# A recurrence and its mixture of experts on one core: step orders written out, the first expert in two passes, four tails in one block

## The chip, the core and the metric

The kernel runs on one core of a Trainium2 chip. A core has TensorE (matmuls; PE in the profile, its weight loads PEld), VectorE (DVE), ScalarE (ACT), GpSimd (POOL) and SyncE (SP), each with an instruction queue of its own that is worked off in order. Data moves by DMA; SP, ACT and POOL start transfers. The metric is the device time of one execution in microseconds (us). A profiled execution also has a span, from its first to its last instruction.

## The reference

The first part is a recurrence over 768 positions for 4 x 8 heads of dimension 40, the second a mixture of eight experts over the 3072 rows that come out, each row going to one expert.

```python
for t in range(S):
    y[:, :, t] = np.einsum('bhd,bhde->bhe', rt, state)
    Sa = np.einsum('bhde,bhe->bhd', state, at)
    state_decay = state * wt[:, :, None, :] - np.einsum('bhd,bhe->bhde', Sa, bt)
    state = state_decay + np.einsum('bhd,bhe->bhde', vt, kt)
...
logits = x @ w_gate                      # x: (3072, 320), 8 experts
expert_idx = np.argmax(logits, axis=1)
...
for e in range(E):                       # rows of one expert
    h = np.maximum(x_sorted[lo:hi] @ w1[e], 0.0)   # 320 -> 1024
    y_sorted[lo:hi] = h @ w2[e]                    # 1024 -> 320
return gate_w[:, None] * y
```

All arithmetic is float32. The inputs come from a fixed seed.

## The kernel before

**Units.** The recurrence is cut into 12 chunks of 64 positions, and the heads into two groups (two of the four batches each). One chunk of one group is a unit: 24 units, numbered in order, and unit u + 2 takes its state from unit u. `unit(u)` (L617) doesn't issue instructions but records steps, each with an engine, what it reads and writes, and a name.

The steps of a unit, by name and engine:
- loads of six inputs, 4 DMA starts each: the decay rows `dec`, then B, K, A, R, V (L642; on ACT for B, A and R of unit 0, on SP otherwise)
- DVE `scan_r` (L658), `recip`, `scan_q` (L664): running products of the decay; POOL `decay_kb` (L670, two) and `decay_a` (L672) apply them to K, B and A
- PE `p_a` (L686): products of the 64 positions with each other; DVE `n1` (L695) masks one half, ACT `gt` and POOL `gt_mask` (L700) the other, DVE `t1` (L716) transposes
- an inverse by doubling: PE `p_sq`, `p_sum2`, `p_sum4`, `p_sum8`, `p_last`, with DVE transposes `x0`, `x02`, `x04`, `x08`, ACT copies `x1`, `x12`, `x14` and sums `s2` (POOL, L720, four), `s4`, `s8` (DVE, L733); each product needs the one before it. The last step into the tile TT is an ACT copy `kept` (three instructions) and a POOL addition `tt_add` (L792)
- PE `p_q`, `p_rhs` (reads the state), `p_u1`, `p_first`, ACT `first`, PE `p_u2`, ACT `minus`, PE `p_z`, DVE `zu` (L907), PE `p_y` (L930, the `ZU,nKB` matmuls), DVE `sa` and POOL `st` (L839, the state for unit u + 2), DVE `xt` (L940)
- PE `p_x` (L953) turns the result to rows and multiplies with the gate's weights; `logits`, `exp`, `weight`, `scaled`, `xs_pad`, and a `store` of the 128 rows to memory. PE transposes are `t_kb`, `t_v`, `t_gt`, `t_st`, `t_u`.

**Order.** `in_order` (L364) issues the steps, greedily, by a planner's costs and ready times. For units 2 to 22 a table `CYCLE` (L312) gives each step a place relative to its unit's number, and each engine but SP takes the steps in the order of these places. Units 0, 1 and 23 and all other steps are placed by the planner.

**Routing.** `route(c0, c1)` (L1011) handles one or two chunks: `choose` (first smallest logit), `p_count` (two f32 matmuls that count rows per expert), `place` (a slot for each row), `one_hots`, `p_table` and an addition to the table `tab` of rows by slot. It is on POOL, and on DVE for the last chunks. After the last chunk `by_count` sorts experts 1 to 7 by their counts, `in_places` reorders the table, and `rows_at` (L233) turns slots into row indices for gathering and scattering. Work on an overflow of rows follows in a branch that runs only if an expert has more rows than its capacity.

**Experts.** An expert's pass has a first layer (`layer1`, 24 matmuls over its columns, that is rows of x; eight of them half as high and run in pairs) and a second (`layer2`, 8 matmuls of 320 columns for each block of 128 rows). Expert 0 runs inside the step planner with the last units: 384 rows gathered by `rows_in` (L1165), transposed by `p_rows` (L1170), first layer, output passes and `rows_out`. Its 64 further rows come with expert 1. Experts 1 to 7, sorted by falling count, have 448, 416, 416, 416, 416, 384 and 384 columns. The rows over 384 are tails; two experts' tails share an output pass (`layer2` with two parts, side by side in the output's partitions), in three shared passes. Weights of the next expert are fetched while one runs; three rooms take turns.

The capacities are in one line:

```python
TAIL = (64, 64, 32, 32, 32, 32, 0, 0)
```

Of the kernel before, what the change touches and what calls it, by code (L numbers as in the profile page):

```python
# [23 lines left out]
def kernel(  # L24
# [23 lines left out]
    nc = tc.nc  # L48
# [27 lines left out]
    TAIL = (64, 64, 32, 32, 32, 32, 0, 0)  # L76
# [43 lines left out]
    before = consts.tile([128, 128], F32)  # L120
    ones_sq = consts.tile([128, 128], F32)
    zero_e = consts.tile([128, E], F32)
    iota_r = consts.tile([128, 128], F16)
    tokv = consts.tile([128, NT], F32)
# [10 lines left out]
    counted("off_b", [128, E], [[PJ * 128, E]], 0, to=offs[:])  # L135
# [7 lines left out]
    def route_constants():  # L143
# [12 lines left out]
        yield lambda: nc.gpsimd.tensor_copy(iota_r[:], iota_f)  # L156
        yield lambda: nc.gpsimd.tensor_copy(tokv[:, : NT // 2], tokc)
        yield lambda: nc.gpsimd.tensor_scalar(tokv[:, NT // 2 :], tokc, scalar1=-1.0, scalar2=None, op0=ALU.mult)
        yield lambda: nc.gpsimd.memset(ptr[:], 0.0)
# [6 lines left out]
    def fill_turn_gate(e):  # L166
        nc.gpsimd.memset(turn_gate[:, :, 2 * D :], 0.0)
        for p in range(NP):
            nc.gpsimd.tensor_copy(
                turn_gate[:, p, : 2 * D].rearrange("x (a d) -> x a d", a=2), ident[:].rearrange("x (a d) -> x a d", a=2)[:, :, :D],  # L170
            )

    def load_turn_gate(e):
        for par in range(2):
            nc.scalar.dma_start(
                turn_gate[par * HP : par * HP + D, :, 2 * D :], moe_w_gate.rearrange("(p a e) n -> a e p n", a=2, e=D)[par],
            )
# [7 lines left out]
    sel = rte.tile([128, NCH, BH, E], F32)  # L185
# [4 lines left out]
    g0_idx = rte.tile([128, NJ], I32)  # L190
    s0_idx = rte.tile([128, NJ], I32)
    g_idx = rte.tile([128, (E - 1) * PJ], I32)
    s_idx = rte.tile([128, (E - 1) * PJ], I32)

    key = rte.tile([128, E - 1], F32)
    over = rte.tile([128, E - 1, E - 1], F32)
# [5 lines left out]
    tab_o = rte.tile([128, (E - 1) * PJ], F32)  # L202

    def by_count():
        v = nc.vector
        v.scalar_tensor_tensor(key[:], in0=ptr[:, 1:], scalar=16.0, in1=iota_f[:, : E - 1], op0=ALU.mult, op1=ALU.subtract)
# [12 lines left out]
    def in_places():  # L219
# [6 lines left out]
        to = tab_o[:].rearrange("x (e j) -> x e j", j=PJ)  # L226
        v.tensor_reduce(to, perm_tab, axis=AX, op=ALU.add)
        v.tensor_copy(to[64:, 0, NJ : NJ + 1], to[:64, 0, NJ : NJ + 1])
        v.tensor_copy(to[:64, 0, NJ : NJ + 1], tab[:64, NJ : NJ + 1])
        for i in (1, 3):  # L230
            v.tensor_copy(to[32:64, i, NJ : NJ + 1], to[:32, i + 1, NJ : NJ + 1])

    def rows_at(v, t, tmp, gi, si):  # L233
# [5 lines left out]
        v.tensor_tensor(tb, tb, ta, op=ALU.add)  # L239
        v.tensor_copy(gi, tb)  # L240

# [1221 lines left out]
```

## Time and profile before

| | us |
|---|---|
| four runs | 698.13 to 705.74, median 702.66 |
| the profiled execution, its own time | 697.83 |
| its span | 696.0 |
| PE busy in the span | 640.9 (92%) |
| PEld, DVE, ACT, POOL busy | 501.5, 389.0, 283.0, 383.8 |
| mean granted TensorE clock | 0.994 of full speed |

Busy times of different engines overlap. The end of a matmul is modelled in the profile, so a busy PE isn't PE at its peak. The first `p_x` (unit 0) starts 58.2 us into the span, those of units 2 and 20 at 91.27 and 394.68, the last at 435.63. Expert 1 begins at 469.25 and the last output pass at 674.92.

### The profile page before, as it was taken

Reading aid. Unit: us, or ns where it says so; the run is one execution under the profiler, and the core shown is the slowest. Engines: PE = TensorE matmul, PEld = TensorE weight load, DVE = VectorE, ACT = ScalarE, POOL = GpSimd, SP = SyncE. Lnnn points to the kernel's source line nnn. Section 1 sums busy time; section 2 is a strip of 40 time slices with the busy share of each in tenths; the row PEclk is TensorE's granted clock in tenths of the full one; section 3 lists DMA queues with packets and bytes.
Section 4 is the critical chain, followed back from the end, with each engine's and each line's share of the span. In section 5 each row is a group of like instructions: output and inputs, shape, how many; then the busy total and the mean of one; then the engine's idle time right before and its main releaser. Section 6 shows DMA issues by size and latency. Waiting matters only on the chain. (4 is left out here: it accounts for less than half of the span.)

```text
span 696.0 us, 32091 instructions
## 1 busy us (share of the span) xinstructions
PE 640.9 (92%) x13957; PEld 501.5 (72%) x13957; DVE 389.0 (56%) x850; ACT 283.0 (41%) x755; POOL 383.8 (55%) x575
## 2 busy tenths in 40 slices
PE   2688989999999999999999987989999999999995
PEld 2477888888889988888888886555746555665653
DVE  5578978888889988887887676701111202010110
ACT  2356656655556655655665654221011101111110
POOL 8788758896889788967895562023115021311101
PEclk9999999999999999999999999999999999999998
DMA  4422323333333333333232101337276019303000
GB/s 101 94 67 60 95 62 77 74 78 98 73 103 81 90 79 75 98 77 92 60 92 65 34 24 50 117 122 240 96 207 208 10 50 288 91 10 94 20 9 25
DMA packets 120212, 60.66 MB, mean 87 GB/s; under 512 B 100587, under 2 KB 115949, under 8 KB 120068
## 3 DMA queue, kind: packets, MB, share of 16 engines
q1 hardware_dynamic: 114696, 48.82, 26.7%
q0 software_dynamic: 2992, 9.25, 4.2%
q8 instruction: 111, 1.82, 1.1%
q10 hardware_dynamic: 2380, 0.50, 0.3%
q14 instruction: 33, 0.27, 0.1%
HBM read 49.88 MB, written 8.98 MB: 85 GB/s over the span
## 5 line engine op out<-in xcount | busy, mean ns | idle before, releaser
L1286 DVE TENSOR_SCALAR h_sb<-hp 128x416 f32<-128x416 f32 (+3 forms) x32 | 17.3, 542 | 188.6 <-PE hp L1281 164.2
L733 DVE TENSOR_TENSOR wx<-ps,wx 64x256 f32<-64x256 f32 (+1 forms) x216 | 90.4, 418 | 41.7 <-PE ps L606 31.4
L606 PE MATMUL ps<-wx 64*64 64x128 f32 (+1 forms) x3072 | 102.1, 266 | 7.5 <-ACT wx L595 1.7
L295 POOL DMA_INDIRECT out_dram<-zo,s_idx x24 | 23.6, 983 | 139.3 <-ACT zo L1303 138.1
L606 PEld LDWEIGHTS ps<-wx 64*64 64x64 f32 x3072 | 80.9, 136 | 19.5 <-issue 8.8
L720 POOL TENSOR_TENSOR wx<-T,ihalf 64x256 f32<-64x256 f32 x96 | 71.3, 743 | 30.5 <-DVE T L716 19.8
L595 ACT COPY wx<-ps 128x256 f32<-128x256 f32 (+2 forms) x124 | 52.2, 422 | 36.3 <-PE ps L606 23.1
L1297 PE MATMUL zp<-w,h_sb 128*128 128x320 f32 (+2 forms) x256 | 66.4, 433 | 0.0
L670 POOL TENSOR_TENSOR KB<-KB,rv 128x512 f32<-128x512 f32 x48 | 58.4, 1220 | 5.6 <-DMA R<-in_packed_dram 1.8
L766 DVE STREAM_TRANSPOSE wx<-ps 128x512 f32<-128x512 f32 x72 | 50.9, 707 | 8.9 <-PE ps L606 6.1
L1297 PEld LDWEIGHTS zp<-w,h_sb 128*128 128x128 f32 (+2 forms) x256 | 41.5, 172 | 18.7 <-issue 3.0
L1287 ACT ACTIVATE h_sb<-hp 128x416 f32<-128x416 f32 (+3 forms) x32 | 15.3, 477 | 93.3 <-PE hp L1281 48.0
L1303 ACT COPY zo<-zp 128x320 f32<-128x320 f32 (+1 forms) x24 | 10.2, 425 | 100.5 <-PE zp L1297 100.5
L1297 PE MATMUL zp<-wx,h_sb 128*128 128x320 f32 (+2 forms) x176 | 48.5, 433 | 0.0
L1273 PE MATMUL hp<-xgT,w 128*128 128x416 f32 (+1 forms) x128 | 46.8, 514 | 0.0
L792 POOL TENSOR_TENSOR TT<-TT,wx 128x512 f32<-128x512 f32 x24 | 34.6, 1442 | 20.6 <-ACT TT L595 18.1
L595 ACT COPY ZU<-ps 64x320 f32<-64x320 f32 x92 | 38.8, 421 | 5.5 <-PE ps L710 4.5
L710 PE MATMUL ps<-ident,Vu 128*128 128x128 f32 x184 | 30.0, 286 | 11.6 <-DMA Vu<-in_packed_dram 11.0
L1297 PEld LDWEIGHTS zp<-wx,h_sb 128*128 128x128 f32 (+2 forms) x176 | 30.9, 178 | 13.4 <-issue 2.6
L606 PE MATMUL ps<-ZU,nKB 128*64 128x104 f32 (+1 forms) x768 | 39.8, 254 | 0.7 <-DVE ZU L907 0.6
L700 POOL TENSOR_TENSOR GT<-GT,m_low 128x512 f32<-128x512 f32 x24 | 31.4, 1310 | 15.9 <-DVE wx L766 9.6
L1251 POOL DMA_INDIRECT xg<-x_rows,g_idx x20 | 19.2, 958 | 37.7 <-PE tp L1259 30.0
(248 smaller groups left out, 1366.5 us busy)
## 6 DMA issues: line engine op xcount, KB each, us to landing
KB<-in_packed_dram SPq DMA_DIRECT2D x188, 40.0 KB
w<-in_moe_w_dram SPq DMA_DIRECT2D x20, 320.0 KB
w<-in_moe_w_dram SPq DMA_DIRECT2D x10, 512.0 KB
x_rows<-xs SPq DMA_DIRECT2D x24, 192.0 KB
dec<-in_packed_dram SPq DMA_DIRECT2D x96, 40.0 KB
Vu<-in_packed_dram SPq DMA_DIRECT2D x96, 40.0 KB
wx<-in_moe_w_dram SPq DMA_DIRECT2D x12, 320.0 KB
A<-in_packed_dram SPq DMA_DIRECT2D x92, 40.0 KB
```

The source lines that it names most:

```text
L295: ins_ = nc.gpsimd.indirect_dma_start(out=out[:, :], out_offset=bass.IndirectOffsetOnAxis(ap=si, axis=0), in_=zo, in_offset=None, bounds_c ...
L595: nc.scalar.copy(dst, src)
L606: nc.tensor.matmul(out_, lhsT=lhsT, rhs=rhs, start=start, stop=stop, skip_group_check=True)
L670: Step(turn_of("decay_kb", pre), POOL, 1.57, lambda e, kb=kb, by=by: nc.gpsimd.tensor_tensor(kb, kb, by, op=ALU.mult), reads=hrv + hKB[2:] ...
L700: Step(turn_of("gt_mask", rk), POOL, 1.33, lambda e, d=dst_, m=mask: nc.gpsimd.tensor_tensor(d, d, m, op=ALU.mult), writes=held)
L710: nc.tensor.transpose(psum[:, ps.at, p * 128 : (p + 1) * 128], t[:, p].rearrange("x a j -> x (a j)"), ident[:])
L720: Step(turn_of("s2", rk + 0.5), POOL, 0.74, lambda e, z=z, par=par, q=q, X=X: nc.gpsimd.tensor_tensor(X[halves[par], q, :, 2, :], T1[halve ...
L733: nc.vector.tensor_tensor(dst[o_, q], src[o_, q], old[o, q], op=ALU.add)
L766: Step(turn_of(f"x0{k}", rk - 0.4), DVE, 0.72, lambda e, ps=ps, Xn=Xn: nc.vector.transpose(Xn[:, :, :, 0, :], half_sums(ps, 2)[:, :, :, 0, ...
L792: Step(turn_of("tt_add", rk - 1.5), POOL, 1.95, lambda e, X=X, TT=TT: nc.gpsimd.tensor_tensor(TT[:], TT[:], X[:, :, :, 2, :], op=ALU.add), ...
L1273: nc.tensor.matmul(hps[i][:, : c1 - c0], lhsT=w[0][:, db, (fb + i) * 128 : (fb + i + 1) * 128], rhs=xT[:, db, c0:c1], start=(db == 0 and n ...
L1297: nc.tensor.matmul(zp[r0 : r0 + n], lhsT=h[:, fb, c0 : c0 + n], rhs=w[2][:, fb, :], start=(fb == 0), stop=(fb == FB - 1), skip_group_check ...
```

## The change

- **Step orders.** `FIRST_STEPS` and `LAST_STEPS` write out, for each engine, SP included, the order of the steps of the first and of the last units, by step, part and unit (`s2/3:1` is the fourth part of `s2` of unit 1). All units take part (`FIRST_UNIT, LAST_UNIT = 0, 23`), `CYCLE` has new places for those between, and routing steps, stores, loads and weight fetches have names and places too.
- **Loads.** For units 0 and 1 half of `dec` is loaded by SP and half by ACT, B by ACT; R of unit 0 by ACT; the rest by SP. The gate's weights are loaded by SP instead of ACT.
- **Engines.** In units 0 to 3 DVE takes one of the two `decay_kb` and two of the four `s2`, in units 0 and 1 also `decay_a`. In the cycle one of two `nkb` goes from DVE to ACT and one of two `x12` from ACT to DVE. In units 0, 1, 22 and 23 TT is formed by DVE straight from PSUM (`direct`) instead of `kept` and `tt_add`.
- **First expert.** 256 of its rows, found in the first 8 of 12 chunks, run inside the planner (`NA = 2`, `EC = 8`); 192 more run as a second pass before expert 1. Eight gathers stand in the planner: two early, two for the second pass, four for expert 1.
- **Tails.** Experts 2 to 5 put their four tails of 32 rows in one block: one gather, one transposition, one `layer2` with four parts. Expert 2's second-layer weights get a tile of their own (`four_w2`), so that they last until expert 5. Expert 7 has 352 columns.
- **Routing.** Slots are placed with an offset per expert of 4096 and fewer operations; counts and selections are in f16 (`p_count`: one matmul and one more for each unit of the group). On DVE the counts are read straight from PSUM. `rows_at` is split into `rows_from` and `rows_to_`. The overflow bookkeeping moves behind expert 3's first layer (`left_over`).

The diff, cut to its core:

```diff
-    TAIL = (64, 64, 32, 32, 32, 32, 0, 0)
+    TAIL = (64, 64, 32, 32, 32, 32, 0, -32)
+    FOUR = range(2, 6)
+    NA = 2
+    EC = 8
...
-    FIRST_UNIT, LAST_UNIT = 2, 22
+    FIRST_UNIT, LAST_UNIT = 0, 23
+    FIRST_STEPS = {
+        PE: """
+            t_v:0 p_a:0 t_kb:0 t_gt:0 p_sq:0 p_a:1 p_sum2:0 t_kb:1 p_sq:1 p_sum4:0 t_v:2 p_rhs:0 p_sum2:1 p_sum8:0 t_v:1 t_gt:1 p_sum4:1 p_last:0
+            p_u1:0 p_first:0 p_q:0 p_sum8:1 p_a:2 p_u2:0 p_rhs:1 p_z:0 t_u:0 t_kb:2 p_last:1 p_sq:2 p_y:0 p_q:1 p_u1:1 p_sum2:2 p_first:1 p_x:0
...
+        DVE: """
+            zero_dec zero_dec/2 zero_dec/1 zero/5 zero/9 zero/10 zero/3 zero/7 zero/1 scan_r:0 scan_r:1 recip:1 decay_kb/1:0 recip:0 scan_q:0
+            decay_a:0 scan_r:2 decay_kb/1:1 n1:0 n1/1:0 t1:0 scan_q:1 decay_a:1 x0:0 s2/1:0 s2/3:0 n1/1:1 n1:1 t1:1 s2/4:0 x02:0 s2/3:1 s2/5:0
+            scan_r:3 x0:1 recip:2 s2/1:1 scan_q:2 x04:0 s4/1:0 s2/4:1 s4:0 x02:1 s2/5:1 s8/1:0 x08:0 s8:0 s4/1:1 direct:0 direct/1:0 s4:1 x04:1
+            decay_kb/1:3 decay_kb/1:2 scan_r:4 n1:2 n1/1:2 s8:1 s8/1:1 x08:1 zu:0 t1:2 zu/1:0 direct/1:1 recip:3 direct:1 s2/1:2 s2/3:2 x0:2 xt:0
...
+        ACT: """
+            first_load/3:0 first_load/1:0 first_load/1:1 pc:0 first_load/3:1 gt/1:0 gt:0 off/1:0 off:0 gk:0 nkb:0 x1:0 nkb/1:0 gt:1 v:0 gt/1:1 pc:2
...
+        SP: """
+            first_load:0 first_load:1 first_load/2:0 first_load/5:0 first_load/4:0 load:2 first_load/2:1 first_load/4:1 load:3 first_load/5:1
...
+    LAST_STEPS = {
+        PE: """
...
+            p_count:21 p_table:19 t_st:23 p_z:23 p_y:22 p_y:23 p_x:22 p_table:21 p_x:23 p_h/13 p_h/14 p_h/8 p_count:23 p_z0/8 p_h/9 p_h/10 p_z0/9
+            p_h/11 p_z0/10 p_table:23 p_z0 p_z0/1 p_h3/2 p_z0/2 p_h/15 p_h3/3 p_z0/11 p_z0/3 p_z0/4 p_z0/5 p_z0/6 p_z0/12 p_rows/3 p_z0/13 p_rows/4
+            p_z0/7 p_rows/5 p_rows/2 p_z0/14 p_rows/6 p_z0/15 p_rows/7
...
-    p_q -0.974  p_last -1.289  p_u1 -0.921  p_first -0.816  p_u2 -0.711  p_z -0.605  p_y -0.342   (places in CYCLE, PE)
+    p_q -0.500  p_last -0.786  p_u1 -0.357  p_first -0.310  p_u2 -0.214  p_z -0.024  p_y  0.167
-    tt_add -2.045  decay_kb -4.955 -5.591  gt_mask -3.136   (POOL)
+    tt_add -0.321  decay_kb -3.393 -3.179  gt_mask -1.250  choose 1.179  place 2.036  one_hots 3.107
...
+                on_ = DVE if spread and q else POOL
...
+                            nc.vector.tensor_tensor(TT[o, q], half_sums(ps, 1)[o_, q, :, 0, :], X[o, q, :, 2, :], op=ALU.add)
...
-                for i, m in enumerate((before, ones_sq)):
-                    mm(psum[:, ps.at, i * n * E : (i + 1) * n * E], m[:], sl_c.rearrange("p b e -> p (b e)"))
+                mm(t[:, :n], before[:], sl_c, stop=False)
+                for b in range(n):
+                    mm(t[:, b + 1 :], ones_sq[:], sl_c[:, b : b + 1].to_broadcast([128, n - b, E]), start=False, stop=b + 1 == n)
...
+    hs[0] = wk_pool.tile([128, FB, CAP - EW], F32, name="h_first", bufs=1)
+    layer1(weights[0], xTs[0], hs[0], EW, CAP, to=0)
+    layer2(rows_to(0, 0), (weights[0], hs[0], 0, 128))
...
+        if p == 1:
+            layer2(rows_to(p, NJ), (weights[0], hs[0], 128, 64), (w, h, MAIN, 64))
+        if p == 3:
+            left_over()
+        if p == FOUR[-1]:
+            layer2(rows_to(FOUR[0], NJ), *((weights[x], hs[x], MAIN, 32) for x in FOUR))
         for j in range(NJ):
-            layer2(rows_to(p, j), (w, h, j * 128, 128))
+            layer2(rows_to(p, j), (w, h, j * 128, min(128, MAIN + TAIL[p] - j * 128)))
```

## The prediction

> **What bounds the kernel now.** I read the table of busy time by stretch first, with cuts where the work changes. Each row is a stretch in us, its length, then the busy us (and instructions) of each engine, the granted clock and the DMA share.
>
> ```profile
> 0.00:91.27 91.27, 66.35 (x1881) 58.30 (x1881) 67.76 (x128) 43.52 (x111) 73.55 (x117) 0.98 0.36 83
> 91.27:394.68 303.41, 290.87 (x9827) 262.20 (x9825) 255.03 (x507) 186.51 (x513) 239.33 (x361) 1.00 0.33 79
> 394.68:436.73 42.05, 35.75 (x1268) 32.06 (x1263) 26.96 (x91) 19.50 (x55) 21.12 (x47) 1.00 0.14 41
> 436.73:469.25 32.52, 29.20 (x117) 18.23 (x115) 11.82 (x71) 8.06 (x22) 6.28 (x8) 1.00 0.38 122
> 469.25:674.92 205.67, 205.67 (x828) 121.74 (x829) 27.48 (x54) 23.68 (x52) 40.56 (x42) 1.00 0.36 112
> 674.92:696.00 21.08, 13.09 (x49) 8.94 (x47) 0.00 (x0) 1.77 (x4) 2.95 (x3) 0.89 0.06 22
> ```
>
> The cuts are the first matmul of `p_x` of units 2 and 20, the end of `p_x` of unit 23, and the first matmuls of expert 1 and of the last output pass. TensorE (first column) bounds it. It is never idle from 469.25 to 674.92, so work removed there shows one for one. In the middle it idles 12.5 of 303 us (a unit takes 16.86 us). The two joints are loose: 24.9 us idle in the first 91, and 6.3 + 3.3 = 9.6 us between 394.68 and 469.25. Next, the timeline of VectorE at the start (start, us, engine, line, operation; in brackets the idle time before it and what ended it).
>
> ```profile
> 6.33 1.24 DVE L658 TENSOR_TENSOR_SCAN rv<-dec,ones 128x521 f32<-128x521 f32 x1
> ...
> 15.58 1.30 DVE L658 TENSOR_TENSOR_SCAN rv<-dec,ones 128x521 f32<-128x521 f32 x1 [4.81 <-DMA dec<-in_packed_dram]
> ...
> 27.73 0.42 DVE L733 TENSOR_TENSOR wx<-ps,wx 128x256 f32<-128x256 f32 x1 [3.49 <-PE ps L606]
> ```
>
> Unit 1's decay rows land 9 us after unit 0's scan, because their load is sixth on SP. Then the waits of TensorE in the second joint (who waited for whom, total us, times, longest):
>
> ```profile
> PE ps L1170 <- DMA qini<-x_rows,g_idx: 3.0, 2, 2.1
> PE ps L606 <- ACT x L601: 1.1, 2, 0.6
> PE ps L606 <- DVE wx L766: 1.1, 1, 1.1
> ...
> PE ps L606 <- DVE xT L940: 0.9, 1, 0.9
> ```
>
> They are the serial steps of the last units and the gathers behind the routing. Last, TensorE's timeline in the expert stage:
>
> ```profile
> 489.23 1.10 PE L1273 MATMUL hp<-xT,w 128*128 128x64 f32 x8
> 490.17 0.82 PE L1259 MATMUL tp<-ident,xg 128*128 128x128 f32 x6
> ...
> 583.51 3.06 PE L1273 MATMUL hp<-xgT,wx 128*128 128x416 f32 x8
> 586.41 0.82 PE L1259 MATMUL tp<-ident,xg 128*128 128x128 f32 x6
> ...
> 629.38 0.43 PE L1297 MATMUL zp<-wx,h_sb 128*32 128x320 f32 x1
> 629.38 0.43 PE L1297 MATMUL zp<-w,h_sb 128*32 128x320 f32 x1
> 629.65 0.43 PE L1297 MATMUL zp<-wx,h_sb 128*32 128x320 f32 x1
> ...
> 644.63 2.85 PE L1273 MATMUL hp<-xgT,w 128*128 128x384 f32 x8
> 647.32 0.82 PE L1259 MATMUL tp<-ident,xg 128*128 128x128 f32 x6
> ```
>
> Start to start, a 416-column matmul instruction takes (586.41 - 583.51) / 8 = 0.362 us and a 384-column one (647.32 - 644.63) / 8 = 0.336: about 0.83 ns a column plus 0.016. Those of 64 columns take (490.17 - 489.23) / 8 = 0.117. The two 32-row tail parts start in the same instant and the next pair 0.27 us later, the same as one full 128-row matmul of the output pass: parts side by side cost one.
>
> **The sum, part by part.** It is made against the profiled execution: span 696.0 us, its own time 697.83.
>
> *Experts (idle-free).* A first-layer pass is 40 instruction slots (32 whole, 16 half-height ones in pairs). Expert 0 had 384 columns (13.4 us) and later 64 (485.19 to 490.17, 4.98). It gets 256 columns, 40 x (0.213 + 0.016) = 9.2, and 192, 40 x (0.160 + 0.016) = 7.0: -2.2 us; nothing is lost, since the output passes stay three and a shared one. Expert 7 goes from 384 to 352 columns: 40 x 32 x 0.83 ns = -1.1. One shared tail pass of 16 pair slots goes, 16 x 0.27 = -4.3, if four parts run side by side as two do. Only pairs are in this trace. Bounds: 0.268 a slot (the pair) and 4 x 0.11 = 0.44 (the weight loads of 128x32 take 0.11; none overlapping), so the four-part pass takes 4.3 to 7.0 and the term is -4.3 to -1.6. I take -4.3: the `ZU,nKB` pass, also 128 rows deep in column halves, does 16 pairs in 1.58 us, so two 128x64 loads fit in 0.1 us and four narrow ones fit in 0.27. One block of transposes less: 525.17 to 525.50, -0.3. Eight gathers instead of seven are turned in the joint: +0.4. Sum of the experts: -7.5.
>
> The Trainium skill ("TensorE: Matmul & The Clock Gate", Measured speedup vs the span model) gives three column tiles a speedup of 2.38 only, so four would not be free; by that efficiency (2.38 / 3) the pass would take an estimated 5.4 us and the term would be -3.2. The pairs of this trace show no such loss.
>
> The counts by expert, worked out from the seeded inputs, are 421, 323, 414, 388, 357, 423, 371, 375. Expert 0 has 293 in the first eight chunks, so 256 early rows are all real. Sorted, the others (423 down to 323) fit 448, four times 416, 384, 352. The overflow branch stays empty.
>
> *Start.* Loads of units 0 and 1 are split over SP and ACT, with unit 1's decay rows second on SP (four starts take 1.6 us there). VectorE takes over half the decay products, part of `s2` and the sum into TT, and becomes the queue that sets the pace. Its list up to `xt:0`, from rows of the profile: fills to 7.3 us; 8 scans x 1.3; 4 reciprocals x 0.2; 6 decay products, new there (0.67, the 128x512 product at L907; the same on POOL takes 1.22); 6 `n1` x 0.42; 9 transposes of T1, x02, x04, x08 x 0.71 and 3 of x0 x 0.68; 6 `s2` halves x 0.42; 8 sums x 0.41 and 8 x 0.86; `zu` 1.34; `xt` 0.69. That is 40.8 us: `p_x:0` at 48.8 with no wait, against 58.2. The lists to `xt:1` and `xt:2` add 11.7 and 18.5, so `p_x:2` comes at 79.0 with no wait, against 91.27: -12.3. VectorE waited 9.4 us for TensorE and 2.7 for ACT in the first 60 us; if all of that is paid again nothing is gained. I take just under half of it, 5.5: **-6.8** (bounds 0 and -12.3). The loads on two queues have no term of their own: one unit's 24 starts take 9.6 us of SP, which VectorE's fills cover to 7.3. ACT's half of unit 0's decay rows stands behind four starts of B, and those behind POOL's KB fill: to about 5.6 us, landing about 7.7, 0.4 late.
>
> *Middle.* A route's two count matmuls in f32 take 0.49 us (395.64 to 396.13). In f16 one more per unit of the group is issued; f16 instructions of 32 columns take 0.05 (four of `oh_c` in 0.19): 5 x 0.05, -0.2, five times -1.0. I summed TensorE's cyclic order in both versions with 15.2 us of pieces a unit. From the end of `p_first` to `p_u2` it has 0.6 us before and 0.9 after, from `p_u2` to `p_z` 0.9 before and 2.0 after; the weight loads waited 3.5 + 0.4 us there for ACT: -3.9. But from `p_last` to `p_q` the cover falls from 4.5 to 3.4 us. That chain is three ACT copies (1.1), possibly a `decay_kb` ahead on POOL (1.22), and `tt_add` (1.28): 2.4 to 3.6. What is queued behind a late `tt_add` is `gt_mask`, the second decay product and `st`, hence the next unit's `p_rhs`. Between 0 and 0.25 us a unit; I take half, +2.0. Middle: **-2.9** (bounds -12.5, all idle time gone, to +4.5).
>
> *Second joint.* Nine of sixteen `p_h` (2 x 0.229 us each) and two `p_h3` now stand among the steps of units 22 and 23: 5 us of filler for 6.3 us idle. Behind `p_x:23` 11.3 us of work stands ahead of `p_rows/3`. The routing there took 13.1 us from 436.83 to the index at 449.91. The DVE list drops 4 + 8 small operations of 0.2, the ACT hop of the counts (0.4) and the 2.6 us of overflow bookkeeping between `by_count` and `tab`; it adds the first index's 0.85 us and a copy: first index after 6.9 us, second after 9.7. Gathers go 1.28 apart and land 3.8 after issue (428.70 to 432.49) up to 6.2 with expert 1's weights in flight (450.65 to 456.89). `p_rows/7` is ready 17.6 to 20 us after `p_x:23`, with 15.6 of work: 2.4 to 4.8 idle, 1.0 more for the copies, and 0 to 3 left among the last units. I take 5.6 instead of 9.6: **-4.0** (bounds -6.5 to 0).
>
> Sum: -7.5 - 6.8 - 2.9 - 4.0 = -21.2. The profiled execution would go from 697.8 to 676.6. The four runs have a median of 702.66, 4.8 above it; I predict against that median: **681**.
>
> **Rivals.**
> - *The start gives nothing.* VectorE's added 4.0 us of decay products and 2.5 us of `s2` halves come while TensorE's pieces run at double length (`p_sum2:0` took 2.19 us, later ones 1.10), so all 12.1 us of waits return. For: those waits are serial steps, which an order can't shorten. Against: in the old order DVE stood idle meanwhile, with unit 1 not loaded. 681 + 6.8 = 688.
> - *The middle tightens.* Every unit falls to the 15.6 us of its pieces: another 9.6 of the 12.5 us idle goes, 671. Against: 10.4 of it is put down to issue, and the order does nothing to that.
> - *Slower: the POOL queue sets the period.* Place: `tt_add`, listed behind `decay_kb` and ahead of `gt_mask`. If `decay_kb` and a routing piece (one `one_hots` pair, 1.1) are both late, `p_q` waits 1.22 + 1.1 + 2.4 - 3.4 = 1.3 us; with `s2` late besides (0.74), 2.1. It is paid 18 times: 38, so 681 - 2 + 38 = 717. It decides from 1.3 us a unit (24 in all). For: POOL is busy 239 of 303 us, and its routing pieces are now fixed in the row. Against: those pieces average less than before, and POOL waited up to 4.8 us for `t1` just where they stand.
> - *The change hardly acts.* Idle time only moves from one hand-off to another, in the units and at both joints, and the experts' work alone goes: 702.7 - 7.5 = 695, or 698 with the four-part pass at its worst; 696 stands for it.
>
> The Trainium skill ("DMA: Bandwidth & Descriptors", Issuing engines are not separate DMA queues) says that issuing from two engines saves only the sequencer's time. By it the split loads do no more than the 0.4 to 1.6 us of issue here; the sum rests on their order anyway.
>
> **Chances.** Forecast 0.56, no gain at the start 0.17, tighter middle 0.12, slower 0.09, hardly acts 0.06. The range is 668 to 697: the low end is the tighter middle with a little more at the start, the high end the case that hardly acts; the four-part pass at its worst (+2.7) is inside. About 1% (7 us) is what a measurement of this kernel tells from no change. Below 695.6 lie the first three and a little of the last: faster 0.86, same 0.05, slower 0.09.
>
> **What would show it.** `p_x:2` near 84, not 91; the spacing of `p_x` near 16.7; idle TensorE between `p_x:20` and expert 1 near 5.6; four `128*32` parts starting together and 16 such groups in 4.3 us; the 352-column pass. A period over 17.5 with TensorE waiting for POOL's TT, or a first `p_x` after 56, would make it wrong.

## The result

| | median us | ratio to the kernel before, 95% interval |
|---|---|---|
| before (78 runs beside it) | 700.7 | 1 |
| after (52 runs) | 702.78 | 1.0017 [1.0001, 1.0033] |
| after, measured again in the experiments | 702.65 | 1.0032 [0.9999, 1.0066] |

The ratio leaves out the slow runs of both kernels, so it isn't quite the quotient of the medians. The forecast was 681, with a range of 668 to 697. The change leaves the time where it was. The profiled execution of the kernel after took 699.47 us, with a span of 697.7 and a mean granted clock of 0.975 (before: 697.83, 696.0 and 0.994).

### The profile page after: what moved, and what is told of

The parts are those of the page before. It is cut to its first block, busy times and chain, and to the rows that moved or that the text cites. A ratio compares the mean times of both kernels' runs of the same rounds, so it can differ in the third digit from the quotient of the medians.

```text
span 697.7 us, 32008 instructions
## 1 busy us (share of the span) xinstructions
PE 640.7 (92%) x13960; PEld 503.2 (72%) x13960; DVE 404.9 (58%) x868; ACT 278.6 (40%) x729; POOL 365.1 (52%) x504
## 4 chain that ended last, share of the span: by engine, by line
PE 46%; issue 30%; POOL 10%; DVE 4%; DMA 1%; ACT 0%; SPq 0%; POOLq 0%
PE ps L715 38%; PE ps L823 6%; POOL out_dram L310 3%; PE ps L944 3%; POOL xg L1396 2%; POOL KB L783 1%; POOL A L785 1%; POOL ST L960 1%; POOL GT L813 1%; POOL wx L833 1%; DMA KB<-in_packed_dram 0%; DVE q L776 0%; SPq L752 0%; PE hp L1418 0%; POOL qini L1301 0%
## 5 line engine op out<-in xcount | busy, mean ns | idle before, releaser
L833 POOL TENSOR_TENSOR wx<-T,ihalf 64x256 f32<-64x256 f32 x88 | 64.8, 737 | 43.1 <-DVE T L829 23.0
L783 POOL TENSOR_TENSOR KB<-KB,rv 128x512 f32<-128x512 f32 x44 | 67.3, 1529 | 15.5 <-DMA KB<-in_packed_dram 15.2
L704 ACT COPY wx<-ps 128x256 f32<-128x256 f32 (+2 forms) x104 | 44.2, 427 | 38.8 <-PE ps L715 17.9
L1449 ACT COPY zo<-zp 128x320 f32<-128x320 f32 (+1 forms) x24 | 10.2, 425 | 101.5 <-PE zp L1443 97.6
L1443 PE MATMUL zp<-wx,h_sb 128*128 128x320 f32 (+3 forms) x176 | 48.5, 434 | 0.0
L1443 PE MATMUL zp<-w,h_sb 128*128 128x320 f32 (+1 forms) x176 | 44.1, 433 | 0.0
L1443 PEld LDWEIGHTS zp<-wx,h_sb 128*128 128x128 f32 (+3 forms) x176 | 30.5, 176 | 13.8 <-issue 0.7
L913 POOL TENSOR_TENSOR TT<-TT,wx 128x512 f32<-128x512 f32 x20 | 26.9, 1346 | 24.1 <-ACT TT L704 20.0
L1418 PEld LDWEIGHTS hp<-xgT,w 128*128 128x128 f32 x128 | 23.7, 190 | 21.1 <-issue 17.1
L770 DVE TENSOR_TENSOR_SCAN rv<-dec,ones 128x521 f32<-128x521 f32 x24 | 37.5, 1566 | 1.8 <-DMA dec<-in_packed_dram 1.4
L1443 PEld LDWEIGHTS zp<-w,h_sb 128*128 128x128 f32 (+1 forms) x176 | 28.9, 176 | 13.2 <-issue 0.7
```

What stands on the lines that cost most here:

```text
L704: nc.scalar.copy(dst, src)
L770: Step(turn_of("scan_r", pre + 0.1), DVE, 1.3 if early else 1.55, lambda e: nc.vector.tensor_tensor_scan(rv[:, : SEG * C1 + 1][:, ::-1], d ...
L783: Step(turn_of("decay_kb", pre), on_, (1.2 if early else 1.35) if on_ == POOL else 0.6, lambda e, kb=kb, by=by: any_(e).tensor_tensor(kb, ...
L833: Step(turn_of("s2", rk + 0.5), DVE if spread and z else POOL, 0.4 if spread and z else 0.74, lambda e, z=z, par=par, q=q, X=X: any_(e).te ...
L913: Step(turn_of("tt_add", rk - 1.5), POOL, 1.6, lambda e, X=X, TT=TT: nc.gpsimd.tensor_tensor(TT[:], TT[:], X[:, :, :, 2, :], op=ALU.add), ...
L1418: nc.tensor.matmul(hps[i][:, : c1 - c0], lhsT=w[0][:, db, (fb + i) * 128 : (fb + i + 1) * 128], rhs=xT[:, db, c0:c1], start=(db == 0 and n ...
```

## The profile after

The table of busy time by stretch, cut at the same places as before (first matmul of `p_x` of units 2 and 20, end of `p_x` of unit 23, first matmul of the expert stage, which is now expert 0's second pass, and of the last output pass). Columns: the stretch, its length, busy us of PE, PEld, DVE, ACT, POOL with instructions, granted clock, DMA share, GB/s.

```profile
0.00:96.28 96.28, 70.56 (x1916) 61.67 (x1917) 79.87 (x148) 43.99 (x112) 54.39 (x104) 0.91 0.33 75
96.28:406.69 310.41, 294.31 (x9954) 263.78 (x9952) 257.27 (x521) 190.41 (x510) 247.28 (x321) 0.99 0.32 78
406.69:443.80 37.11, 36.06 (x1130) 31.33 (x1129) 28.96 (x77) 12.68 (x36) 13.20 (x29) 1.00 0.12 34
443.80:469.17 25.37, 19.06 (x79) 12.58 (x77) 10.56 (x69) 5.69 (x19) 7.36 (x9) 0.87 0.54 173
469.17:676.00 206.83, 206.83 (x839) 124.91 (x840) 27.88 (x55) 24.05 (x52) 39.97 (x41) 1.00 0.35 111
676.00:697.70 21.70, 13.86 (x52) 8.97 (x50) 0.32 (x1) 1.74 (x4) 2.91 (x3) 0.89 0.06 21
```

Three things stand out. The first row ends at 96.28, not at 91.27, although POOL is busy 19 us less: VectorE took that work over (67.8 to 79.9 us). TensorE idles about as long as before (25.7 us, before 24.9), so most of the 5.0 us lost is busy time (70.6 us, before 66.4); part of it is the clock, as 21.8 us of that busy time lie ahead of the clock's first rise or in stretches where it was halved (17.2 before). The clock column doesn't show this rightly: it counts the time ahead of the first rise (20.46 us here, 32.68 before) as full, though pieces ran at double length there. The fourth row loses 6.3 us of TensorE's time and has a clock of 0.87. And the expert stage is as full as before.

The places of the cuts make a sum against the forecast's own terms (the forecast span was 674.8). Unit 18 is taken as the third cut here, because the order of the last units changed:

| stretch | before | forecast | after | after - forecast |
|---|---|---|---|---|
| start, to `p_x:2` | 91.3 | 84.5 | 96.3 | +11.8 |
| 16 units, to `p_x:18` | 269.2 | 266.6 | 267.2 | +0.6 |
| second joint, to the expert stage | 108.8 | 96.4 | 105.7 | +9.3 |
| experts, to the end | 226.8 | 227.3 | 228.5 | +1.2 |

(The experts' forecast has the 192 columns and one output pass that moved there.) The prediction failed in the start and the second joint, by 21 of 22.9 us.

**The start.** The timeline of SP, of ACT and of VectorE in the kernel after:

```profile
24.40 1.58 SPq L752 DMA_DIRECT2D A<-in_packed_dram  x4
26.03 13.69 SPq L752 DMA_DIRECT2D KB<-in_packed_dram  x4
39.81 1.53 SPq L752 DMA_DIRECT2D R<-in_packed_dram  x4
...
37.62 1.54 ACTq L752 DMA_DIRECT2D R<-in_packed_dram  x4
...
48.49 1.91 DVE L783 TENSOR_TENSOR KB<-KB,rv 128x512 f32<-128x512 f32 x2 [3.63 <-DMA KB<-in_packed_dram]
```

Four DMA starts take SP 1.5 to 1.6 us; those of unit 2's K take 13.69. The table of SP's waits says for what:

```profile
SPq L752 <- DMA R<-in_packed_dram: 10.9, 1, 10.9
```

It is the R of unit 0, a load on the *other* queue into another buffer. The program's instruction list shows why: the transfers that SP and ACT start signal on the same eight completion counters in turn, and a start waits until the transfer that used its counter last has landed. The fourth start of unit 2's K has the counter of the first start of unit 0's R. R stands 17th in ACT's list, behind copies that wait for TensorE, and starts at 37.62. Until it has landed SP starts nothing, and the loads behind it come some 10 us late (R of unit 1 starts at 39.81; with R of unit 0 early, below, at 29.20); VectorE, which has unit 3's product listed ahead of unit 2's, waits 3.63 us.

**The second joint.** TensorE's waits from `p_x:20` on, then the gathers on POOL, the weights on SP and TensorE's timeline:

```profile
PE ps L1310 <- DMA q<-x_rows,g_idx: 5.2, 2, 3.2
PE hp L1418 <- ACT rv L704: 1.1, 1, 1.1
```

```profile
450.25 1.14 POOL L1301 DMA_INDIRECT q<-x_rows,g_idx  x1 [3.52 <-DVE g_idx L252]
451.69 0.94 POOL L1301 DMA_INDIRECT q<-x_rows,g_idx  x1 [0.30 <-issue]
453.76 0.94 POOL L1301 DMA_INDIRECT q<-x_rows,g_idx  x1 [1.12 <-DVE xe L1389]
...
450.16 0.95 SPq L298 DMA_DIRECT2D wx<-in_moe_w_dram  x2
...
458.62 0.52 PE L1310 MATMUL ps<-ident,q 128*128 128x128 f32 x3 [3.19 <-DMA q<-x_rows,g_idx]
461.68 0.90 PE L1310 MATMUL ps<-ident,q 128*128 128x128 f32 x3 [2.00 <-DMA q<-x_rows,g_idx]
```

The first index came 6.1 us after the last logits, where 6.9 were forecast. But the gathers issued at 450.25 and 451.69 are used 8.4 and 10.0 us later, not 3.8 to 6.2: expert 1's weights start at the same moment, and 173 GB/s move in this stretch (before 122). Behind the idle time pieces take double: three transpositions 0.90 us instead of 0.52.

**The experts.** TensorE's timeline of the new pieces:

```profile
469.17 1.57 PE L1418 MATMUL hp<-xT,w 128*128 128x192 f32 x8 [1.12 <-ACT rv L704]
...
476.57 4.47 PE L1443 MATMUL zp<-w,h_first 128*128 128x320 f32 x16
...
619.37 0.43 PE L1443 MATMUL zp<-w,h_sb 128*32 128x320 f32 x1
619.38 0.43 PE L1443 MATMUL zp<-wx,h_sb 128*32 128x320 f32 x1
619.38 0.43 PE L1443 MATMUL zp<-w,h_sb 128*32 128x320 f32 x1
619.39 0.43 PE L1443 MATMUL zp<-four_w,h_sb 128*32 128x320 f32 x1
619.64 0.43 PE L1443 MATMUL zp<-w,h_sb 128*32 128x320 f32 x1
...
664.14 2.53 PE L1418 MATMUL hp<-xgT,wx 128*128 128x352 f32 x8
666.61 1.46 PE L1426 MATMUL hp<-xgT,wx 64*128 64x352 f32 x8
```

Four parts start within 0.02 us, the next four 0.27 later. A 352-column slot takes (666.61 - 664.14) / 8 = 0.309 (worked out: 0.308), and the 192-column pass 7.4 us (7.0).

## The experiments

All are edits of the kernel after unless another is named; "ratio" is to the kernel before on the same chip. Theory A: the losses are head-of-line waits that can be named (SP behind R, small index operations ahead of a sum, gathers beside weights). The rivals differ by place and stand in the expectations.

**R of unit 0 early.**

```diff
 ACT:   pc:0 first_load/3:1 +first_load/6:0 gt/1:0 ...  x12/1:1 x12:1 -first_load/6:0 gk:1
 POOL:  decay_kb:0 zero/8 +zero/2 ...  gate/2 -zero/2 gate/3
```

> Changed against the kernel after: unit 0's load of R stands 5th instead of 17th on ACT, and the zero fill of its buffer moves up in POOL's list. Nothing else moves. Theory A (SP is held by ACT): the fourth start of unit 2's K on SP waits for the completion of R's load, because the loads of both queues share a few completion semaphores in turn; R starts at 37.62 us and SP stands from 28.4 to 39.2. With R early SP's wait of 10.9 us on R goes, unit 2's and 3's K and B start by about 30 to 36 instead of 39 to 47, VectorE's 3.63 us and POOL's 12.75 us behind KB shrink to under 1 and 5, p_a of unit 2 comes 3 to 6 us before its 50.45, and p_x of unit 2 at 86 to 91 instead of 96.28: 5 to 10 us less in all, 693 to 698 against a kernel after of 702.8. Theory B (VectorE is simply full at the start with the products that it took over): SP is free, p_x of unit 2 stays between 94 and 97, and the time moves by less than 2 us.

Measured: 696.29 us, ratio 1.0003 [0.9971, 1.0035]; the profiled span fell from 697.7 to 692.5. SP's timeline:

```profile
27.41 1.70 SPq L752 DMA_DIRECT2D KB<-in_packed_dram  x4
29.20 1.55 SPq L752 DMA_DIRECT2D R<-in_packed_dram  x4
```

The 13.69 us are gone, VectorE's wait for KB fell from 3.6 to 1.4 us and POOL's from 15.2 to 0.4. `p_x` of unit 0 comes at 59.2 instead of 62.0 and that of unit 2 at 92.28 instead of 96.28. Over all kernels with the written start and VectorE's new share, `p_x:2` lies at 92.3 to 94.4 with this edit (five, mean 93.1) and at 94.9 to 96.8 without it (seven, mean 95.8). The total times don't tell a gain from none (the interval overlaps that of the kernel after). So the wait of one queue on the other is real, but by these traces it is worth 2 to 4 us, mean 2.7, and not theory A's 5 to 10. The start is then near where it was before the change (91.27), not at 84.5.

**Unit 2's product ahead of unit 3's.** `decay_kb/1:3 decay_kb/1:2` exchanged in VectorE's list.

> Changed against the kernel after: in VectorE's list the decay product of unit 2 stands ahead of that of unit 3 (they stood the other way round). SP stays held as it is. Theory A: VectorE no longer waits 3.63 us at 48.49 for unit 3's load in front of unit 2's ready data (landed about 41.5); p_a of unit 2 starts at about 47 instead of 50.45 and p_x of units 0 and 2 come 2 to 4 us earlier (62.02 to about 59, 96.28 to about 93); the wait of 10.9 us on SP is still there. About 700. Theory B (VectorE is full): no difference over 1 us, p_x of unit 2 at 95 to 97.

Measured: 699.2 us, ratio 1.0013 [0.9971, 1.0055]; `p_x` of units 0 and 2 at 60.43 and 94.90. That is 1.4 us under the kernel after, but only 0.2 under the lowest of the executions without the edit (95.1 to 96.8). So a cost of VectorE's own order isn't told from none; the late load is what it waits for.

**Less work on VectorE.** On top of `r_early`, units 2 and 3 give `decay_kb/1`, `s2/1` and `s2/3` back to POOL's list.

> R of unit 0 early as in r_early, and for units 2 and 3 the second decay product and two of the four s2 halves go back from VectorE to POOL, as the kernel before had them (POOL stood idle from 38.7 to 51.9 us in r_early). Theory B (VectorE is the queue that sets the start: 79.1 us of work up to xt of unit 2 in r_early and in the kernel after, against 66.6 in the kernel before): its work falls by 3.0 us and p_x of unit 2 comes 2.5 to 4 us earlier than 92.28, at 88 to 90. Theory C (its waits for TensorE and ACT set the pace, the work only fills them): p_x of unit 2 moves by less than 1 us, or comes later because POOL's s2 halves take 0.72 us each instead of 0.44.

Measured: 699.86 us, ratio 0.9996 [0.9965, 1.0027]. Up to `p_x:2` VectorE is busy 77.1 us instead of 80.1, but `p_x:2` comes at 96.45, later than in `r_early`. The 2.5 to 4 us of theory B did not come. Its waits grow instead: 12.0 us for `n1` and `wx` behind TensorE and ACT, against 5.4. So the amount of VectorE's work alone doesn't set the start. The run doesn't tell what less work would give without more on POOL.

**TensorE's clock at the start.** On the last version below (`best2`), 28 and 12 transpositions of the identity that nobody reads:

```diff
 PE:  +warm t_v:0 +warm/1 p_a:0 t_kb:0 t_gt:0 ...
```

> best2 with 28 transpositions of the identity ahead of TensorE's first piece of work (it stands idle until 10.4 us) and 12 between the first transposition of V and p_a of unit 0 (3.6 us idle). Theory I (the clock follows how busy TensorE has been): the full clock is granted earlier than at 24 us, the pieces of unit 0 between 15 and 25 us take about 1.1 us for 64x128 instead of 2.0 to 2.2, and p_x of units 0 and 2 come 1 to 3 us earlier than in best2 (59 and 92.7). Theory J (the first clock rise has a fixed time, or the start is set by the chain over VectorE, ACT and POOL, whose pieces don't depend on TensorE's clock): p_x of unit 0 within 0.7 us of best2.

Measured: 692.33 us, ratio 0.9886 [0.9838, 0.9934], against 0.9859 without it. TensorE's timeline with the added pieces, and then that of `best2`:

```profile
1.88 4.58 PE L1253 MATMUL ps<-ident 128*128 128x128 f32 x28 [1.88 <-POOL ident masks.py:199]
10.12 0.63 PE L829 MATMUL ps<-ident,Vu 128*128 128x128 f32 x4 [3.67 <-DMA KB<-in_packed_dram]
...
14.95 2.21 PE L721 MATMUL ps<-KB,A 64*64 64x128 f32 x32 [2.40 <-POOL col_b_i L160]
```

```profile
10.61 1.09 PE L829 MATMUL ps<-ident,Vu 128*128 128x128 f32 x4 [10.61 <-DMA A<-in_packed_dram]
15.11 2.23 PE L721 MATMUL ps<-KB,A 64*64 64x128 f32 x32 [3.41 <-issue]
```

The clock did rise early (the same four transpositions take 0.63 instead of 1.09 us; the granted clock is full from 4.6 us), and fell again at 11.4, behind 3.67 us of idle time: `p_a` takes 2.2 us in both. `p_x` of units 0 and 2 come at 59.65 and 93.42 (`best2`: 60.66, 94.36; two other kernels with the same start: 58.9 to 59.0 and 92.7 to 92.9). No gain; but as the full clock didn't last to `p_a`, the run doesn't tell what a full clock from there on would be worth. Neither SP's stall alone nor less work on VectorE brings the start below 92. What keeps it there stays open: the clock, or the serial chain over all four engines, whose hand-offs no run shortened.

**The first list left out.**

```diff
-    FIRST_UNIT, LAST_UNIT = 0, 23
+    FIRST_UNIT, LAST_UNIT = 2, 23
+    FIRST_STEPS = {}
```

> The kernel after without the list of the first units alone: units 0 and 1 are placed by the planner, units 2 to 22 by the new cyclic places, the last units by their new list. VectorE keeps its products of units 0 to 3. Theory A (the list's loads and order cost the start 4 to 5 us): p_x of unit 2 at 90 to 93 instead of 96.3, and 3 to 5 us less than the kernel after, ratio to the kernel before 0.994 to 0.999. Theory F (the new cycle, in which decay products come 1.5 to 2 units later, needs the list's head start): p_x of units 2 and 3 come later than 96 and 111, and it is slower than the kernel after.

Measured: 705.93 us, ratio 1.0077 [1.0049, 1.0106]. `p_x` of unit 0 at 71.84, of unit 2 at 98.03. Theory A's numbers missed and theory F's signs came out (unit 3 at 115.28): with the work on VectorE the planner's own start is worse than the list with its stall. That it is the new cycle that needs the list wasn't tried.

**The old places, with the new experts and routing.** No lists, the cyclic places of the kernel before (without those of loads and stores), `spread = False`, `decay_a` on POOL.

> The kernel after with the old places: the lists of the first and last units are left out, the cyclic places are those of the kernel before (loads and stores left to the planner), and in units 0 to 3 the decay products and s2 are POOL's again. What stays new: the experts' part (256 and 192 rows, four tails in one block, 352 columns) and the routing's code. It tells the experts' work from the orders. Theory D (the experts' work saves its 7.5 us wherever the order stands, and the new orders give all of it back): 693 to 697 where the kernel before has 702, ratio 0.987 to 0.994, p_x of unit 2 at 90 to 93. Theory E (the eighth gather and the moved pass wait at the joint, whatever the order): the same as the kernel before within 2 us, ratio 0.997 to 1.003.

Measured: 710.69 us, ratio 1.0144 [1.0088, 1.02]. Both theories missed. The units take 17.25 us instead of 16.8, and expert 0's second pass begins at 478.44. Loads without places, the direct sum into TT and the new routing are all in it, so this run doesn't separate the experts' work from the orders; it only shows that the new pieces in the old places are slower than either kernel.

**The four tails as two pairs**, one behind the other into the same block.

```diff
-        for fb in range(FB):
+        for side, fb in [(side, fb) for side in range(0, len(parts), 2) for fb in range(FB)]:
```

> The kernel after with the four tails of 32 rows run as two pairs, one pair behind the other, into the same output block. If four parts side by side cost the same as two (0.27 us a group, as its trace has it), 16 groups more: the expert stage from the second pass of expert 0 to the end is 4.3 us longer (228.5 becomes 232.8), nothing else moves. If the narrow weight loads were the bound, the two pairs would cost as much as the four together and nothing changes.

Measured, one run (709.56 us in all): from expert 0's second pass to the end 231.8 us instead of 228.5, +3.3. The trace explains the missing 1.0: the last 4 of the first pair's 16 groups ran beside the first 4 of the second pair's (both start at 629.09), as the two pairs write different partitions.

```profile
628.82 0.43 PE L1443 MATMUL zp<-w,h_sb 128*32 128x320 f32 x1
628.82 0.43 PE L1443 MATMUL zp<-four_w,h_sb 128*32 128x320 f32 x1
629.09 0.43 PE L1443 MATMUL zp<-w,h_sb 128*32 128x320 f32 x1
629.09 0.46 PE L1443 MATMUL zp<-wx,h_sb 128*32 128x320 f32 x1
629.09 0.43 PE L1443 MATMUL zp<-four_w,h_sb 128*32 128x320 f32 x1
```

Four parts cost what two cost, and the pass that was saved is worth its 16 x 0.27 us less that overlap.

**The early indices later.**

```diff
 DVE:  s2/5:21 v:22 +rows_from:15 s4/1:21 x04:21 +rows_to:15 n1/1:22 ...
```

> Changed against the kernel after: the row indices of the first 256 gathered rows (11 small VectorE operations) are not computed in one piece at 381.15 to 386.29 ahead of the sums of unit 21, but four of them behind the copy of V of unit 22 and seven behind a transpose, where VectorE waits for TensorE. Theory A (the small operations stand in front of a sum that TensorE waits for, and wait themselves for POOL): TensorE's wait of 3.19 us at 387.20 falls under 1 us, the half clock from 385.8 to 392.6 goes, the small operations take 0.2 us each instead of 1.1 where POOL is idle, and p_x of unit 20 (406.69) comes 4 to 6 us earlier; 697 to 699 in all against 702.8. Theory B (the unit's own chain is the limit there, the order on VectorE isn't): another wait takes its place and p_x of unit 20 moves by less than 1.5 us.

The kernel after computes the first 256 row indices on VectorE at 381.15, in front of a sum; beside POOL's work three of the first four small operations take about 1.1 us instead of 0.2 (timeline of VectorE, POOL and TensorE in the kernel after):

```profile
382.26 1.09 DVE L250 SCALAR_TENSOR_TENSOR idx_tmp<-tab,idx_tmp 128x2 f32<-128x2 f32 x1
384.07 1.10 DVE L252 TENSOR_TENSOR g_idx<-idx_tmp,idx_tmp 128x2 int32<-128x2 f32 x1
385.21 0.17 DVE L257 TENSOR_SCALAR idx_tmp<-g_idx 128x2 int32<-128x2 int32 x1
...
382.16 1.18 POOL L783 TENSOR_TENSOR KB<-KB,rv 128x512 f32<-128x512 f32 x1
383.98 1.18 POOL L785 TENSOR_TENSOR A<-A,q 128x512 f32<-128x512 f32 x1
...
387.20 1.76 PE L715 MATMUL ps<-wx 64*64 64x128 f32 x26 [3.19 <-DVE wx L846]
```

The Trainium skill ("SBUF — State Buffer", SBUF: two separate sides) says that a VectorE operation with two inputs in SBUF and a GpSimd operation that reads SBUF lock each other out for a whole instruction. The 1.1 us beside 1.18 and the 0.17 behind them agree in size; a one-input operation (L249) took 1.08 us here too.

Measured: 698.29 us, ratio 0.9996 [0.9952, 1.004]. The wait of 3.19 us and the half clock are gone, but from `p_x:18` to `p_x:23` it takes 76.8 us against 79.2 in the kernel after and 77.2 when that was run again, where the clock happened to stay full. Waits of 1.26, 1.18 and 1.12 us stand in its place. Counted to `p_x:20` the gain is 3.8 us against the kernel after, but 0.8 against that kernel run again. Over all kernels with the new last list, `p_x:18` to `p_x:23` takes 76.0 to 79.4 us with the edit (six, mean 77.4) and 76.2 to 83.5 without it (nine, mean 78.6). So a gain isn't told from none; theory B is nearer.

**Weights behind the second indices.** The three operations that make `order_i` (L226 to 228) become a step of their own, `by_order:23`, behind `rows_from/1:23`.

> Changed against the kernel after: the three operations that tell SP which weights expert 1 needs run behind the second block of row indices, so that the fetch of 2.6 MB starts at about 454 instead of 450.16, behind the first two gathers and not ahead of them. Theory A (the gathers are slow because the weights' transfers fill the DMA engines): the gathers issued at 450.25 and 451.69 land in 3.8 to 5 us instead of 8 to 10, TensorE's waits of 3.19 and 2.00 us shrink to under 2 together, the half clock from 460.9 to 467.7 goes, and the second pass of expert 0 starts at 463 to 466 instead of 469.17: 3 to 6 us less, unless the later gathers are held up instead. Theory B (the gathers take 8 us for their own descriptors): the waits stay, and the start moves by less than 1 us. If the weights come too late, TensorE waits at expert 1, at about 481, which shows in the trace.

Measured: 696.37 us, ratio 0.9991 [0.9944, 1.0039]. The weights start at 453.50; TensorE's waits for the first late gathers fall from 3.19 and 2.00 to 0.35 us, and 2.47 come back at the fourth. From the first late gather to the second pass it is 15.7 us instead of 18.9: 3.2 gained, theory A. The total time doesn't tell it from the kernel after.

**Four edits together:** R early, late indices, late weights, and the overflow bookkeeping made to depend on expert 3's first layer. Though written behind that layer, it was emitted among the routing's last operations (L1374 to L1389, from 448.3 to 453.6).

> Four edits together: R of unit 0 early, the early row indices behind V of unit 22, expert 1's weights behind the second indices, and the overflow bookkeeping made to depend on expert 3's first layer, so that it can't be emitted earlier. If the losses are separate, as their traces say, their gains add: -3 at the start (p_x of unit 2 at 92), -4 at the early indices, -3 at the late gathers, and -1 for the bookkeeping (the second index 8.5 us behind the logits instead of 9.6): 11 less than the kernel after, 687 to 690, and 1.2 to 1.8% under the kernel before. If a gain is taken back where the next wait is (as the wait of a unit in its state), 693 to 697.

Measured: 697.41 us beside 702.65 for the kernel after in the same round, ratio 0.9951 [0.9919, 0.9982]. 5.2 us gained of the 11 hoped for. The third gather is issued 2.7 us behind the first instead of 3.5, so the bookkeeping cost 0.9. But the fourth gather now meets the weights: TensorE waits 3.57 us for it, and the clock is halved from 457.4 to 467.6.

**The same with POOL's share back.**

> The edits of fixed and of pool_kb together. Theory B: 3 us under fixed, so 684 to 687. Theory C: as fixed within 1 us.

Measured: 697.78 us, ratio 0.998 [0.9949, 1.0011]. No gain, theory C again.

**Weights behind the last gather.** On `fixed`, two small operations are added that make the order of the experts depend on the last gathered block, and all of them stand behind `rows_to:23` (`gathers_first`).

> As fixed, and SP learns which weights expert 1 needs only when the last of the eight gathers has landed, so no transfer of weights runs beside a gather (in fixed the third to sixth late gathers still met it: 451.32 to 458.21, a wait of 3.57 us and half the clock from 457.5 to 467.7). Theory A (the weights slow the gathers): each late gather lands in 3.5 to 5 us, TensorE's waits ahead of the second pass of expert 0 fall from 4.7 us to under 2, the half clock there goes, the second pass starts 3 to 5 us earlier against p_x of unit 23, and the time is 692 to 695 where fixed had 697.4, ratio 0.986 to 0.991. Theory G (gathers take 6 us anyway, one after the other): the waits stay, no gain. Too late weights would show as a wait of TensorE in expert 1's first layer, 12 us behind the start of the second pass.

Measured: 694.34 us, ratio 0.9934 [0.9904, 0.9964]. No gather waits for the weights: the last one, issued at 451.54, has landed by 454.80, 3.3 us. From the first matmul of `p_x:23` to the second pass it is 20.8 us (26.5 in the kernel after, 24.1 in `fixed`); the total times of `fixed` and this run aren't told apart. What is left is the copy of the first output block, which now stands on VectorE behind the operation that waits for that gather (2.10 us), and a half clock from 457.6 to 464.4.

**That copy exchanged with ACT's** (`best2`: `zo` to ACT, `zo/1` to VectorE).

> As gathers_first, with the two copies of expert 0's output blocks exchanged between VectorE and ACT: the first block's copy no longer stands behind the three small operations that wait there for the last gather. Theory A (that copy's place alone makes TensorE wait 2.10 us for rv at 455.89, and the half clock from 457.7 follows): the wait falls under 0.5 us and the second pass of expert 0 starts 2 us earlier against p_x of unit 23 (20.8 us behind it in gathers_first); if the half clock goes too, 690 to 693 where gathers_first had 694.3, ratio 0.984 to 0.990. Theory H (the clock halves there whatever the waits are): 2 us less at most.

Measured: 690.89 us (6 runs), ratio 0.9859 [0.9812, 0.9906]: 1.4% faster than the kernel before, the fastest of all. The row of the table by stretch that answers to 443.80:469.17 of the kernel after:

```profile
443.90:461.18 17.28, 16.16 (x78) 10.66 (x76) 9.33 (x55) 5.78 (x19) 7.43 (x10) 1.00 0.33 101
```

The same pieces take 16.16 us of TensorE instead of 19.06, because the clock is 1.00, and 1.1 us of idle time are left of 6.3. Against `gathers_first` 2.1 us of waiting went, and the second pass, which ran its first pieces at half clock there (2.92 us for eight instead of 1.57), got the full clock too. From `p_x:23` to the end of the execution that makes 4.0 us. Not all that was won since the kernel after stays: the weights now start at 461.50, beside the second pass; that pass has a wait of 1.37 us at 466.47, and from its start to the end it takes 230.3 us instead of 228.5. Whether the late fetch is the cause wasn't tried.

**Is it the idle time that halves the clock?** In the kernel after, 24 and 14 unread transpositions of the identity in TensorE's list ahead of the first two late gathers' pieces, no wait removed.

```diff
 PE:  ... p_z0/12 +warm p_rows/3 p_z0/13 +warm/1 p_rows/4 ...
```

> The kernel after with 24 and 14 transpositions of the identity, whose result nobody reads, in TensorE's list ahead of the transpositions of the first and second late gather, where TensorE waits 3.0 to 3.2 and 1.1 to 2.0 us. They add work and take no wait away. Theory I (the clock halves because TensorE stood idle): the half clock from 460.9 to 467.7 goes, and what follows (p_rows, the last output pieces) runs at full length; the second pass starts up to 2 us earlier, or at the same time if the added pieces outlast the waits. Theory J (the clock halves there for another reason, as the weights' transfers): the half clock stays at the same place though TensorE is busy.

Measured: 699.09 us, ratio 0.9971 [0.9932, 1.001].

```profile
452.06 2.78 PE L1245 MATMUL ps<-ident 128*128 128x128 f32 x24
455.70 0.55 PE L1319 MATMUL ps<-ident,q 128*128 128x128 f32 x3 [0.86 <-DMA q<-x_rows,g_idx]
```

The row of the table by stretch around them has a clock of 1.00, with 190 GB/s moved:

```profile
440.60:463.70 23.10, 20.55 (x117) 14.86 (x115) 10.55 (x69) 5.68 (x18) 7.37 (x9) 1.00 0.60 190
```

With 4.5 us of useless work added, the half clock at this place is gone and the second pass comes 24.2 us behind `p_x:23` instead of 26.5 (25.4 when the kernel after was run again). The weights still start beside the first gather (446.94 and 447.03), whose rows are used 8.7 us after issue (8.4 in the kernel after). So it is the idle time, theory I, and not the transfers. It is one trace; of the other executions with the new last list, only `best2` and `warm_start`, which is built on it, have no half clock here. The ratio points the same way, but its interval overlaps that of the kernel after.

The Trainium skill ("TensorE: Matmul & The Clock Gate", Why this matters for your kernels) warns of idle gaps over about 3 us. These runs show less: at the early indices waits of 1.23 and 1.43 us close together were enough (`pool_kb`), or 0.96 and the first 0.6 of 1.71 (`swap_kb`), while 0.69 and 2.26 were not in the kernel after run again. By that rule the 2.10 us in `gathers_first` should have been harmless; the half clock followed 1.7 us behind.

## Why the prediction was wrong

- *Experts: right.* Terms of -4.3 for the tails, -1.1 for 352 columns and 7.0 for 192 columns measured 16 x 0.27, 0.309 us a slot and 7.4. The estimate of 5.4 us for a four-part pass from the Trainium skill's 2.38 is not borne out.
- *Start: wrong by 11.8.* Two steps failed most. One is "The loads on two queues have no term of their own": VectorE waited 4.6 us for loads up to `xt:2` (2.5 with R early). Two queues that share completion counters can stop each other, and that cost 2 to 4 us. The other is the step from `xt:2` to `p_x:2`, taken as 0.7 us: `p_x:2` starts 3.5 us behind it, as TensorE has pieces of units 3 to 5 listed in front. The work of VectorE was nearly right (fills to 7.3 and 71.0 us more), but came out 2.4 us longer, with the pauses under 0.15 us between operations counted in: the six decay products took 6.4 us instead of 4.0, one scan of 1.24 took 2.93. The term "I take just under half of it, 5.5" for waits for TensorE and ACT was mis-sized by 2.0: they came to 7.5 (6.1 with R early). And VectorE as "the queue that sets the pace" isn't borne out: less work on it gave nothing. The rival with no gain at the start comes nearest; the start was 5.0 us longer than before.
- *Middle: open.* 267.2 us instead of 269.2 looks like the forecast 266.6, but 15 executions with the same middle lie between 265.4 and 271.5, mean 268.6. A gain of 2.6 can't be told from none there. The slow rival (POOL's addition) didn't come: no mean period over 17.0.
- *Second joint: wrong by 9.3.* The second index came as worked out (9.6 us, forecast 9.7), the first 0.8 us sooner (6.1). Wrong were the gathers' landing, "3.8 after issue up to 6.2" (8.4 and 10.0 beside the weights), the bookkeeping counted as gone (0.9 us, it was still there), and idle time "5.6 instead of 9.6" (7.4 from `p_x:20` on, and the 3.2 of the early indices ahead of it, in a place where none was expected). Moving filler to before `p_x:23` left less of it behind, where the waits now fell; what that alone cost wasn't tried. `best2` reaches 95.9 us in this stretch, where 96.4 was forecast: the forecast for it was reachable, not reached.
- *No term for the clock.* Idle stretches were priced as idle time alone, and some were paid again in half clock: TensorE is busy 640.7 us in the kernel after and 634.9 in `best2`, with the same experts and units. Of these 5.8 us, 2.9 lie between `p_x:23` and the second pass.

The time came out between the rival that "hardly acts" (696) and the slower one (717): the experts' work was saved, and the two joints gave it back.

## What to carry to other kernels

A load that is listed late on one queue can stop the loads of another queue, through completion counters that both use; look in the queue's own waits for a tensor that the waiting transfer has nothing to do with. Price a wait of TensorE of about 2 us as the wait and up to as much again for the halved clock behind it (`gathers_first` against `best2`: 2.1 us of waiting, 4.0 in all). A gather that others wait for goes ahead of a bulk fetch of weights, not beside it; here that order, with a copy moved out of the way and the edits of `fixed`, turned a change of no effect into 1.4%.

## What was not expected of the hardware

- The clock halved in stretches of 3.4, 6.8 or 10.2 us at waits whose longest was 1.4 to 3.6 us, but not at all of them. In `warm_start` it rose 2.7 us after the first added transposition (1.88 to 4.60); in `best2`, where waits break up the first work, 16 us after the first piece (10.61 to 26.61).
- Useless matmuls in a wait brought the next stage 1.2 to 2.3 us nearer, at a place where the clock would have halved. That the whole time fell with it (ratio 1.0032 or 1.0017 to 0.9971) isn't clear of the noise.
- Small VectorE operations of 0.17 us took 1.1 beside POOL's, one scan of 1.24 took 2.93.
- Rows of an indirect gather of 128 were there 3.3 us after issue without the weights' fetch, and were used 8 to 10 us after issue beside the 2.6 MB of weights.
